# Attention and expert layers in one kernel: the third chunk's value products moved three steps earlier in 17 of 48 units, and two small copies moved to VectorE

## The chip, the cores and the metric

The kernel runs on one core of a Trainium2 chip. The metric is the device time of one launch in microseconds (us); a measurement is the median over several runs. Engines are called by their names or as the profile writes them: PE is TensorE's matmul side, PEld its weight loads, DVE is VectorE, ACT is ScalarE, POOL is GpSimd, SP is SyncE, which only issues transfers here.

## What is computed

Attention with normalised queries and keys over 8 batches, 12 heads, 448 positions and a head width of 64, then a gated expert layer of 8 experts, each token going to one of them.

```python
q_n, k_n = (rmsnorm(q, g_q), rmsnorm(k, g_k))
scores = scale * np.matmul(q_n, k_n.transpose(0, 1, 3, 2))
scores = scores - np.max(scores, axis=-1, keepdims=True)
attn = np.exp(scores)
attn = attn / (np.sum(attn, axis=-1, keepdims=True) + 1e-09)
attn_out = np.matmul(attn, v)
...
e_idx = np.argmax(x @ w_gate + modality_bias[modality_id], axis=1)
h = np.maximum(x[mask] @ w1[e], 0.0)
out[mask] = gate_w[mask, None] * (h @ w2[e])
```

The change touches the attention part alone.

## The kernel before, in words

**Units and steps.** The attention runs over 48 units (`NU`), a unit being two heads of one batch. The order of all work is written out by hand: a table `plan`, filled by `put(n, ...)`, says at which step `n` a piece is issued, and one loop walks the steps. A unit has seven steps, so `n = 7 * i + j` with the unit `i` and the step `j` from 0 to 6. The order in which a step's pieces are called is the order on each engine, and each engine runs its own in that order; the only freedom left at run time is how long an engine waits for a semaphore.

**What a step does.** The 2 x 448 positions of a unit's keys make seven chunks of 128 rows. In step `j`, `st(i, j)` (line 1012) multiplies chunk `j` of the keys with all queries into a bank of PSUM from the pool `ps_s`, which has two banks, and ACT turns the bank into exponentials (`A.activation(... Exp)`, line 1023). The third score product after a given one overwrites the bank of the first, so it has to wait for that exponential. Chunk 3 holds the last 64 rows of the first head and the first 64 of the second and takes four matmuls instead of two. In the same step `sa` (line 981) makes a chunk of a coming unit's scores, in the chunk order 3, 0, 1, 2, 4, 5, 6, only for their row maxima: DVE reduces each (`V.tensor_reduce`, line 994), again over two banks (`ps_a`). Step 3 and step 0 of the next unit also transpose queries and keys of a coming unit (`tr`, line 902): four PE transposes, a rounding copy by ACT, and a difference by DVE that waits for that copy; ACT then lays rounded rows into the operands, by four copies that come right after the exponential of step 4.

**The value products.** `av(u, c)` (line 1051) multiplies the exponentials of unit `u` with its values, during the steps of unit `i = u + 1`. Chunks `c` = 0, 1 and 2 are pairs of products, one for each head, on one half of the array's columns each; each product is recorded as two PE matmuls, so a pair is four of them. Chunk 3, shared by the heads, is one product over the full array, from a block-diagonal copy of the values.

```python
PLAN = {..., 'av': (1, 1, 4, 6), ...}
put(NJ * (u + 1) + (AVJ[c] if u < NU - 2 else min(AVJ[c], 6)), "av", u, c)
```

So chunks 0 and 1 are issued in step 1, chunk 2 in step 4 and chunk 3 in step 6. In step 4 there may follow `sums` (line 1078; after every odd `u`) or `gates` (line 1087; after every fourth `u`, here 8, 12, ... 40), eight matmuls of 32 columns each, four at a time side by side; and then `xt` (line 1122), four transposes. ACT empties the gates' bank before the exponential of step 5.

**The shared values.** `values(u)` (line 1064) fills the block-diagonal operand for chunk 3 by two copies of 64 x 64 within SBUF. It is called at the end of step 2 of unit `u + 1`, so on its engine it stands between step 2 and step 3.

**Other work around it.** POOL normalises queries and keys (two products of 1.05 us in a row at about step 2 or 3) and adds up exponentials; DVE also finishes `xt` (line 1131), and in every sixth unit the routing of a batch (`route_top`, line 1163, six small operations after step 4's reduction).

Of the kernel before, what the change touches and what calls it, by code (L numbers as in the profile page):

```python
# [21 lines left out]
NJ = 7  # L22
NP = H // 2
NU = B * NP
# [42 lines left out]
def kernel(  # L67
# [15 lines left out]
    V, A, G = (Deferred(e, n) for e, n in ((nc.vector, "op"), (nc.scalar, "act"), (nc.gpsimd, "dma")))  # L83
# [352 lines left out]
    def view(t, off, p, *dims):  # L436
        n = 1
        for d in dims:
            n *= d
        a = t[:p, off : off + n]  # L440
        if len(dims) > 1:
            ax = " ".join("abcd"[: len(dims)])
            a = a.rearrange(f"p ({ax}) -> p {ax}", **dict(zip("abcd"[1:], dims[1:])))
        return a
# [27 lines left out]
    vd_b = [view(at_l, 8 * DM - 128 * (i + 1), 128, 128) for i in range(2)]  # L472
# [336 lines left out]
    if True:  # L809
# [8 lines left out]
        HB = {}  # L818
# [244 lines left out]

        def values(u):
            for h, r in enumerate((LO, HI)):
                A.copy(vd_b[u % 2][r, 64 * h : 64 * h + 64], HB[u // 3]["v"][r, u % 3, 3])

        def avcopy(u):
            t = T[u]
# [305 lines left out]
        def put(n, *what):  # L1375
            plan.setdefault(n, []).append(what)

        P = PLAN
        AVJ, XTJ, XTE, SMJ, LAJ, RCJ = (P[x] for x in ("av", "xt", "xte", "sm", "la", "rc"))
# [7 lines left out]
        def xt_at(u):  # L1387
            if u < NU - 8:
                return NJ * (u + 6) + XTJ
            return NJ * (NU - 2 + (u - NU + 8) // 2) + XTE[u % 2]  # L1390

        def when(what, u):
            return P["first"].get((what, u), NJ * u - P[what])

        for u in range(NU):
            for j in range(NJ):
                jj = ((0, 1, 2, 4, 5, 6, 3) if u < P["early"] else (3, 0, 1, 2, 4, 5, 6))[j]
                put(when("sa", u) + j * (P["sastep"] if u == 0 else 1), "sa", u, jj)
            put(when("mt", u), "mt", u)
            if u < NU - 1:  # L1400
                for c in range(4):
                    put(NJ * (u + 1) + (AVJ[c] if u < NU - 2 else min(AVJ[c], 6)), "av", u, c)
            put(xt_at(u), "xt", u)
            if u % 2:
                put(NJ * (u + 1) + (SMJ if u < NP * (B - 2) else P["sml"]), "sums", u - 1)
            if u % 4 == 3:
                put(NJ * (u + 2) + (LAJ if u < NP * (B - 2) else min(LAJ, 4)), "gates", u // 4)
                put(NJ * (u + 2) + (RCJ if u < NP * (B - 2) else min(RCJ, 6)), "recips", u // 4)
            put(when("tk", u), "tr", u, 1)
            put(when("tq", u), "tr", u, 0)  # L1410
            put(when("nq", u), "norm", u, 0)
            put(when("nk", u), "norm", u, 1)
            put(when("sk", u), "sq", u, 1)
            put(when("sq", u), "sq", u, 0)
            if ("rs", u) in P["first"]:
                put(when("rs", u), "rs", u // 3, P["rs0"].get(u, 0), u % 3 + 1)
            elif u > 8 and u % 3 == 2:
                put(when("rs", u), "rs", u // 3, 0, 3)
            if 5 < u < 10:
                put(when("ld", u), "load", u)  # L1420
            elif u > 9 and u % 2 == 0:
                put(when("ld", u) - 1, "load", u, 2, (0,))
                put(when("ld", u) + 1, "load", u, 2, (1,))

        for n in range(P["start"], NJ * NU):
# [63 lines left out]
            if 0 <= i < NU and j in CSJ:  # L1489
                h = CSJ.index(j)  # L1490
# [20 lines left out]
            if i > 0 and j == 2:  # L1511
                values(i - 1)
            if i == NU - 1 and j == 4:
                values(i)
# [45 lines left out]
        u, g = NU - 1, NU // 4 - 1  # L1560
# [187 lines left out]
```

## Time and profile before

| what | value |
|---|---|
| median of 3 runs | 1034.41 us (1032.71 to 1034.77) |
| the profiled execution | 1034.98 us |
| its span in the trace | 1033.3 us |
| PE busy | 1013.8 us, 98% of the span |
| PE weight loads busy | 818.9 us, 79% |
| DVE, ACT, POOL busy | 743.5, 709.0, 715.9 us (72%, 69%, 69%) |
| granted TensorE clock | 0.998 of full speed |
| attention units | from about 26 to 540 us of the span |

The profiled execution is 1.7 us longer than the span of its instructions, and 0.6 us above the median of the runs. In the 40 slices of the page PE stands at 9 tenths nearly throughout, and ACT and DVE at 7 to 9 tenths up to the middle of the span, so busy shares alone don't tell what a shorter PE step would bring: a busy PE is one that has matmuls in flight. The trace's timeline, with the start of each matmul, tells more.

### The profile page before, as it was taken

The numbers are of one execution on the slowest core, as the hardware profiler recorded it, in microseconds if no ns is written. First come the engines' busy times: TensorE is split into PE (matmuls) and PEld (weight loads), VectorE is DVE, ScalarE is ACT, GpSimd is POOL, SyncE is SP. The second block draws the span as 40 slices with busy tenths as digits, with TensorE's granted clock in tenths as the row PEclk, the third lists the DMA queues.
The fourth block names the chain that finished last, engine by engine and source line by source line (L and its number), as shares of the span: only waits on it lengthen the run. The fifth ranks groups of instructions, "written<-read, shape, count | busy, mean of one in ns | idle before, by whom it ended". The sixth has DMA issues, their size and how long they took to land. (4 is left out here: it accounts for less than half of the span.)

```text
span 1033.3 us, 18863 instructions
## 1 busy us (share of the span) xinstructions
PE 1013.8 (98%) x6462; PEld 818.9 (79%) x6462; DVE 743.5 (72%) x1260; ACT 709.0 (69%) x1379; POOL 715.9 (69%) x747
## 2 busy tenths in 40 slices
PE   9899999999999999999989999999999999999997
PEld 7655666666666666656559999999999999999995
DVE  6777888887888788886667986755685567556740
ACT  7897999889999899888655555545554455545531
POOL 7788798989788887889856646865545554565361
PEclk9999999999999999999999999999999999999999
DMA  8776667868677786766748506144572342234162
GB/s 197 187 170 138 153 141 183 178 141 185 160 168 162 160 186 148 167 116 126 228 121 286 94 20 195 32 123 123 150 279 66 119 123 79 65 105 123 40 210 92
DMA packets 147900, 148.20 MB, mean 143 GB/s; under 512 B 72702, under 2 KB 137682, under 8 KB 147284
## 3 DMA queue, kind: packets, MB, share of 16 engines
q1 hardware_dynamic: 122398, 105.08, 43.0%
q0 software_dynamic: 25328, 41.82, 12.8%
q8 instruction: 53, 0.87, 0.4%
q14 instruction: 51, 0.42, 0.2%
q10 hardware_dynamic: 70, 0.02, 0.0%
HBM read 150.31 MB, written 33.39 MB: 178 GB/s over the span
## 5 line engine op out<-in xcount | busy, mean ns | idle before, releaser
L609 PE MATMUL ph<-xw,w1w 128*128 128x256 f32 x2016 | 246.1, 284 | 1.7 <-ACT at_w2lw L52 0.8
L609 PEld LDWEIGHTS ph<-xw,w1w 128*128 128x128 f32 x2016 | 243.9, 192 | 3.3 <-issue 1.1
L52 DVE TENSOR_REDUCE at_hlw<-sa 128x1 f32<-128x448 f32 x336 | 205.1, 619 | 26.3 <-PE sa L991 24.7
L1019 PE MATMUL st<-w1w 128*128 128x448 f32 (+1 forms) x480 | 183.5, 432 | 2.4 <-ACT at_w2lw L52 1.1
L52 POOL DMA_INDIRECT r<-in_moe_w_dram,tb_w x60 | 84.0, 1399 | 53.4 <-DVE w1w L52 38.1
L52 ACT ACTIVATE hhw<-ph 128x512 fp32r<-128x512 f32 x56 | 33.5, 597 | 121.2 <-PE ph L609 121.2
L639 PE MATMUL py<-w2lw,hhw 128*128 128x384 f32 x448 | 113.8, 335 | 0.0
L52 ACT ACTIVATE r2w<-st 128x448 f32<-128x448 f32 x168 | 91.0, 544 | 32.8 <-PE st L1019 26.6
L52 DVE TENSOR_TENSOR w1w<-r,w1w 128x768 fp32r<-128x768 f32 x112 | 103.9, 958 | 11.0 <-ACT w1w L52 9.9
L991 PE MATMUL sa<-w1w 128*128 128x448 f32 (+1 forms) x288 | 108.0, 375 | 3.6 <-DVE at_hlw L52 3.3
L52 POOL DMA_INDIRECT r2w<-in_moe_w_dram,tb_vi x48 | 50.0, 1041 | 84.7 <-DVE w2lw L52 75.7
L52 ACT CAST w1w<-xw 64x448 fp32r<-64x448 f32 x188 | 105.8, 563 | 3.7 <-issue 1.4
L52 DVE TENSOR_TENSOR w2lw<-r2w,w2ha 128x1536 fp32r<-128x1536 f32 x28 | 49.1, 1757 | 81.0 <-ACT w2ha L52 81.0
L1019 PEld LDWEIGHTS st<-w1w 128*128 128x128 f32 (+1 forms) x480 | 86.1, 190 | 25.5 <-issue 10.7
L1019 PE MATMUL st<-w1w,w2ha 65*128 65x448 f32 x288 | 100.5, 369 | 0.0
L52 POOL TENSOR_TENSOR r2w<-r2w 128x448 f32<-128x448 f32 (+1 forms) x72 | 82.9, 1152 | 24.0 <-DVE r2w L52 15.1
L52 ACT ACTIVATE at_w2lw<-st 128x448 f32<-128x448 f32 x168 | 90.6, 544 | 12.1 <-PE st L1019 6.9
L52 POOL TENSOR_TENSOR xrw<-r,at_hlw 112x512 f32<-112x512 f32 x95 | 97.6, 1047 | 0.5
L52 ACT CAST w1w<-r 128x768 fp32r<-128x768 f32 x112 | 95.3, 904 | 0.1
L52 ACT ACTIVATE yw<-py,ltn 128x384 f32<-128x384 f32 x55 | 29.3, 578 | 79.1 <-PE py L639 75.5
L639 PEld LDWEIGHTS py<-w2lw,hhw 128*128 128x128 f32 x448 | 80.9, 188 | 0.0
L52 POOL TENSOR_TENSOR r2w<-r2w,at_w2lw 64x448 f32<-64x448 f32 (+1 forms) x48 | 54.7, 1140 | 31.3 <-DVE r2w L52 15.7
(302 smaller groups left out, 2208.1 us busy)
## 6 DMA issues: line engine op xcount, KB each, us to landing
w1w<-xw SPq DMA_DIRECT2D x216, 112.0 KB
xg<-xrw SPq DMA_DIRECT2D x14, 768.0 KB
xrw<-xg SPq DMA_DIRECT2D x56, 192.0 KB
r<-in_q_dram SPq DMA_DIRECT2D x19, 448.0 KB
r<-in_k_dram SPq DMA_DIRECT2D x19, 448.0 KB
w2ha<-xw SPq DMA_DIRECT2D x72, 112.0 KB
w1w<-w1w SPq DMA_DIRECT2D x48, 112.0 KB
r2w<-in_v_dram SPq DMA_DIRECT2D x24, 224.0 KB
```

What stands on the lines that cost most here:

```text
L52: return fn(*a, **kw)
L609: PE.matmul(ps[:, i], lhsT=lt_, rhs=rt_[:, c], start=n == 0, stop=n == 17)
L639: PE.matmul(ps[n][:, :384], lhsT=lt_[:, j, 128 * t : 128 * t + 128], rhs=rt_[:, 384 * n : 384 * n + 384], start=j == 0 and m == 0, stop=j ...
L991: PE.matmul(ps[:, :S], lhsT=t["qq"][r, h, a : a + 128], rhs=t["kk"][h][r], start=True, stop=True)
L1019: PE.matmul(ps[:, :S], lhsT=l, rhs=t["qq"][:, h] if first else t["ql"][0:65, h], start=first and (j != 3 or h == 0), stop=not first and (j ...
```

## The change

```diff
         def values(u):
             for h, r in enumerate((LO, HI)):
-                A.copy(vd_b[u % 2][r, 64 * h : 64 * h + 64], HB[u // 3]["v"][r, u % 3, 3])
+                copy = V.tensor_copy if 8 <= u < 42 else A.copy
+                copy(vd_b[u % 2][r, 64 * h : 64 * h + 64], HB[u // 3]["v"][r, u % 3, 3])
...
                 for c in range(4):
-                    put(NJ * (u + 1) + (AVJ[c] if u < NU - 2 else min(AVJ[c], 6)), "av", u, c)
+                    aj = AVJ[1] if c == 2 and u % 2 == 0 and 8 <= u < 41 else AVJ[c]
+                    put(NJ * (u + 1) + (aj if u < NU - 2 else min(aj, 6)), "av", u, c)
```

In the 17 units 8, 10, ... 40 chunk 2's four PE matmuls move from step 4 to step 1, behind those of chunks 0 and 1. For the 34 units 8 to 41 the two copies of the shared values move from ACT to DVE, at the same place between steps 2 and 3. Nothing else moves.

Three places show it. All rows are of the products of unit 26 in the steps of unit 27, the number behind a name being the scheduler's own (`av` the value products, `st` the scores, `sa` those for the maxima, `tr` and `xt` transposes). On PE, before:

```order
L1061 MATMUL av_3860<-r2w 64x448 x4
L1002 MATMUL mt_3865<-idn,at_hlw 7x128
L1019 MATMUL st_2_3875<-w1w 128x448 x2
L991 MATMUL sa_1_3878<-w1w 128x448
L1019 MATMUL st_3_3891<-w1w 128x448 x4
L991 MATMUL sa_2_3896<-w1w 128x448
L910 MATMUL tr_0_3898<-idn,xrw 128x112 x4
L1019 MATMUL st_4_3906<-w1w 128x448 x2
L991 MATMUL sa_4_3909<-w1w 128x448
L1061 MATMUL av_3860<-r2w 64x448 x2
L1127 MATMUL xt_3913<-idn,at_hhw 112x128 x4
```

and with the change:

```order
L1061 MATMUL av_3860<-r2w 64x448 x6
L1002 MATMUL mt_3867<-idn,at_hlw 7x128
L1019 MATMUL st_2_3877<-w1w 128x448 x2
L991 MATMUL sa_1_3880<-w1w 128x448
L1019 MATMUL st_3_3893<-w1w 128x448 x4
L991 MATMUL sa_2_3898<-w1w 128x448
L910 MATMUL tr_0_3900<-idn,xrw 128x112 x4
L1019 MATMUL st_4_3908<-w1w 128x448 x2
L991 MATMUL sa_4_3911<-w1w 128x448
L1128 MATMUL xt_3913<-idn,at_hhw 112x128 x4
```

The two products of chunk 2 have left the place between `sa_4` and `xt` and lengthen the group in front of `mt`; the rows between are the same.

On ACT, from the exponential of step 2 (`st_2`) to that of step 5, with the change (before, one row more stood behind the first: `COPY at_w2lw<-r2w 64x64 x2`):

```order
L52 ACTIVATE at_w2lw<-st_2_3877 128x448
L52 ACTIVATE at_w2lw<-st_3_3893 128x448
L52 CAST xw<-tr_0_3900 128x448
L52 ACTIVATE at_w2lw<-st_4_3908 128x448
L52 CAST w1w<-xw 64x448
L52 CAST xw<-xw 64x64
L52 CAST w1w<-xw 64x448
L52 CAST xw<-xw 64x64
L52 ACTIVATE at_w2lw<-st_5_3937 128x448
```

The four casts still stand between the exponentials of step 4 and of step 5.

On DVE, the same steps with the change (before, the row with COPY was not there):

```order
L52 TENSOR_REDUCE at_hlw<-sa_1_3880 128x1
L52 COPY at_w2lw<-r2w 64x64 x2
L52 TENSOR_REDUCE at_hlw<-sa_2_3898 128x1
L52 TENSOR_TENSOR w1w<-tr_0_3900,xw 128x448
L52 TENSOR_REDUCE at_hlw<-sa_4_3911 128x1
L52 TENSOR_REDUCE ra_3925<-lo_3808 112x4
```

The two copies now stand between the maxima of chunks 1 and 2, and what follows them is as before.

## Rows read from the trace of the kernel before

**Rows 1.** Busy time by stretch: us, then PE, PEld, DVE, ACT, POOL, PEclk, DMA.

```profile
240.00:320.00 80.00, 80.00 (x443) 50.02 (x443) 67.07 (x129) 72.34 (x169) 67.98 (x74) 1.00 0.75 170
```

**Rows 2.** Timeline of PE in unit 27: start, length, operation, count.

```profile
314.25 1.72 PE L1061 MATMUL av<-r2w 128*64 128x448 f32 x8
315.91 0.28 PE L1002 MATMUL mt<-idn,at_hlw 128*7 128x128 f32 x1
...
318.49 0.37 PE L991 MATMUL sa<-w1w 128*128 128x448 f32 x1
318.79 0.97 PE L1061 MATMUL av<-r2w 128*64 128x448 f32 x4
319.69 0.65 PE L1127 MATMUL xt<-idn,at_hhw 128*112 128x128 f32 x4
...
321.21 0.37 PE L991 MATMUL sa<-w1w 128*128 128x448 f32 x1
321.41 0.91 PE L1057 MATMUL av<-r2w,at_w2lw 128*128 128x448 f32 x2
321.81 0.71 PE L1019 MATMUL st<-w1w 128*128 128x448 f32 x1
...
322.56 0.37 PE L986 MATMUL sa<-xw 128*128 128x448 f32 x1
```

**Rows 3.** Timeline of PE at the attention's end, chunks 0 to 2 together.

```profile
536.77 2.48 PE L1061 MATMUL av<-at_w2lw 128*64 128x448 f32 x12
539.18 1.02 PE L1057 MATMUL av<-at_w2lw 128*128 128x448 f32 x2
```

**Rows 4.** Timeline of PE in unit 25, where gates follow.

```profile
297.04 0.37 PE L991 MATMUL sa<-w1w 128*128 128x448 f32 x1
...
298.24 0.57 PE L1090 MATMUL sm<-at_hhw,wg 128*32 128x448 f32 x2
...
299.13 0.65 PE L1127 MATMUL xt<-idn,at_w2hb 128*112 128x128 f32 x4
```

**Rows 5.** Timeline of ACT in unit 27, from step 4's exponential to step 5's.

```profile
318.69 0.55 ACT L52 ACTIVATE at_w2lw<-st 128x448 f32<-128x448 f32 x1
...
320.45 0.24 ACT L52 CAST xw<-xw 64x64 fp32r<-64x64 f32 x1
320.84 1.16 ACT L52 ACTIVATE at_w2lw<-st 128x448 f32<-128x448 f32 x2 [0.15 <-PE st L1019]
```

**Rows 6.** Timeline of PE in unit 37, step 4's score product.

```profile
422.47 0.47 PE L1019 MATMUL st<-w1w 128*128 128x448 f32 x1
```

**Rows 7.** Timeline of ACT in unit 37, step 2's exponential.

```profile
421.90 0.52 ACT L52 ACTIVATE at_w2lw<-st 128x448 f32<-128x448 f32 x1
```

**Rows 8.** Timeline of DVE in unit 27.

```profile
316.85 0.63 DVE L52 TENSOR_REDUCE at_hlw<-sa 128x1 f32<-128x448 f32 x1
317.87 0.62 DVE L52 TENSOR_REDUCE at_hlw<-sa 128x1 f32<-128x448 f32 x1 [0.40 <-PE sa L991]
318.82 0.62 DVE L52 TENSOR_TENSOR w1w<-tr,xw 128x448 fp32r<-128x448 f32 x1 [0.33 <-ACT xw L52]
...
321.60 1.15 DVE L52 TENSOR_REDUCE at_hlw<-sa 128x1 f32<-128x448 f32 x2
322.67 0.67 DVE L52 SCALAR_TENSOR_TENSOR r2w<-at_w2lw,half 128x448 f32<-128x448 f32 x1
```

**Rows 9.** The routing's first small operation on DVE, 80 to 430 us: count, ns, times.

```profile
L52 DVE TENSOR_REDUCE ra<-lo x5: 182/184/186, 152.4 to 403.5; 112x4 f32<-112x32 f32 x5
```

**Rows 10.** Groups of DVE copies after 1000 us: count, busy us, mean ns.

```profile
L52 DVE COPY xrw<-idn 32x32 f32<-32x32 f32 x4 | 0.4, 283 | 0.0
```

**Rows 11.** Timeline of DVE in unit 19: the operation with two SBUF inputs.

```profile
238.60 1.60 DVE L52 SCALAR_TENSOR_TENSOR r2w<-at_w2lw,half 128x448 f32<-128x448 f32 x1
```

**Rows 12.** Timeline of POOL at that time, and in unit 27.

```profile
238.58 1.14 POOL L52 TENSOR_TENSOR r2w<-r2w,at_w2lw 64x448 f32<-64x448 f32 x1
...
316.51 2.05 POOL L52 TENSOR_TENSOR xrw<-r,at_hlw 112x512 f32<-112x512 f32 x2
318.52 1.14 POOL L52 TENSOR_TENSOR r2w<-at_w2lw 128x448 f32<-128x448 f32 x1
```

## Prediction

> **What bounds the kernel now.** I first read the busy time by stretch: in the middle of the attention PE is busy for the whole of 80 us, while ACT stands at 72 and DVE at 67 [rows 1]. So PE is the bound there, and a shorter PE sequence would shorten the kernel one for one, as long as the others keep up. A busy PE only has matmuls in flight, though, so I went on to the timeline and read start against start. The change touches 17 units, in each at two places: the group of value products in step 1 and the one in step 4. The third view is the timeline of ACT and DVE beside it, for what follows PE there: 72 of 80 us is little room for an engine that has to answer PE within two score banks.
>
> **What the moved products save on PE.** Unit 27 stands for the plain units, in which no gates follow.
> - Step 4 before: from the maxima product to the transposes behind the value products 318.49 to 319.69, 1.20 us [rows 2]. A maxima product followed by a product over the full array takes 321.21 to 321.41, 0.20 [rows 2]. Taking the group out frees 1.00 us.
> - Step 1: eight matmuls take 314.25 to 315.91, 1.66 [rows 2]. Twelve of the same kind, at the end of the attention, take 536.77 to 539.18, 2.41 [rows 3]. So the third pair costs 0.75 there.
> - Net 0.25 us less: what is saved is one way into the half-array form and out of it again.
>
> Where gates follow (9 of the 17: 8, 12, ... 40) the way from the maxima product to the gates' first matmul is the same 1.20, 297.04 to 298.24 [rows 4]. But the gates split the array too, into quarters. Their own way in, straight from a full-array product, the trace of these steps doesn't show; the value group's is 318.49 to 318.79, 0.30 instead of 0.20 [rows 2]. The bounds are 0.20 and 0.30, the saving 0.25 or 0.15. I take 0.15, since both are the same switch from whole to split. If PE were all, the sum would be 8 x 0.25 + 9 x 0.15 = 3.35 us less, at most 17 x 0.25 = 4.25.
>
> **What the later steps 2 to 4 cost.** All between the two places now starts 0.75 later, while what follows step 4 is to start 0.25 earlier. ACT and DVE lose 1.00 us between them in every such unit. In unit 27 they follow PE closely: DVE waited 0.40 for PE, then 0.33 for ACT's copy of the transposes [rows 8]. So they shift by the whole 0.75 (bounds 0 and 0.75; 0 only with a backlog that would hide the shift, and these waits exclude one).
> - ACT: step 4's exponential goes from 318.69 to 319.44. The four casts end at 320.45 + 0.24 = 320.69 and left 0.15 us of idle time before step 5's exponential [rows 5]; now they end at 321.44. Step 5's exponential, 0.55 long like step 4's [rows 5], runs until about 322.01.
> - The next unit's first score product overwrites that bank. A product waiting for such an exponential starts 0.05 behind it: 421.90 + 0.52 = 422.42, and 422.47 [rows 6, 7]. So it starts at 322.06, where PE would be ready at 321.81 - 0.25 = 321.56 [rows 2]. **PE stalls 0.50 and the unit ends up 0.25 longer than before, not 0.25 shorter.**
> - DVE: its difference of the transposes goes from 318.82 to 319.57. Behind it no idle time is printed up to the two reductions at 321.60 [rows 8], since this is a unit with the six small routing operations. The first ends at 322.22, now 322.97. The maxima product at 322.56 [rows 2] needs that bank and could start at 323.02: 0.46 later than before, not 0.25. The routing falls into 5 of the 8 plain units, the first at 152.4 and the last at 403.5 [rows 9]. In the other three DVE has that much less to do, and the 0.25 stands.
> - Where gates follow, they take 298.24 to 299.13, 0.89 us of PE [rows 4], ahead of step 5. That covers nearly all of the 1.00, so the saving of 0.15 stays.
>
> **The two copies.** ACT loses two short copies between the exponentials of steps 2 and 3. In the moved units ACT waits there for PE, which is later now, so this can't shorten the chain above; in the others nothing on PE waits for ACT. I cost it at nothing; its cover is PE's own full row, and if ACT were the bound in those units, it would be a gain. DVE gains two copies of 64 x 64. The trace has no such copy; the nearest is one of 32 x 32, four of which keep DVE busy for 0.4 us, mean 283 ns [rows 10]. So two cost 0.2 to 0.6 us; I take 0.3. They stand in the 0.40 us in which DVE waited for PE [rows 8], which hides them, and the later PE adds 0.36 behind them in the moved units. That is zero as long as they don't have to wait.
>
> **Sum.** 5 x 0.45 + 3 x 0.25 - 9 x 0.15 = 2.25 + 0.75 - 1.35 = **1.65 us more**. On the profiled execution (1034.98) that is 1036.63; that one lies 0.57 above the median of the runs, so the median becomes 1034.41 + 1.65, about **1036.0 us**. A step that moves 17 groups then moves the kernel by less than 0.2% (2.07 us), about what a measurement of this kernel can tell from no change.
>
> **Rivals.**
> - *Faster: ACT keeps up.* If step 5's exponential in the plain units ends by 321.51, PE finds its bank free at 321.56 and all savings stay: 3.35 us less, 1031.1 us. It decides at a lateness of ACT of 0.25 instead of 0.75. For it speaks that ACT loses 0.5 us of copies and had 0.15 idle [rows 5]. Against it: the copies stand ahead of the place where ACT waits for PE, and the four casts can't pass each other.
> - *Slower: DVE's copies wait for POOL.* An operation of DVE with two inputs in SBUF took 1.60 us beside a POOL operation of 1.14 that had begun just before [rows 11, 12], and 0.67 where POOL left it alone [rows 8]. If a copy within SBUF is held up likewise, then in the plain units with routing: DVE is free for the copies at 316.85 + 0.63 + 0.75 = 318.23, POOL's second product runs until 318.56, and the addition behind it begins at once, 1.14 long [rows 12]. If the first copy goes in between and the second waits for the addition, DVE reaches chunk 2's reduction at about 320.06 and the difference at 320.68 instead of 319.57. The 1.1 us go through to the maxima product of the next unit: 5 x 1.1 more, 1034.41 + 1.65 + 5.5 = 1041.5 us. It decides at a delay of the copies of about 0.7 us; a single wait of 0.33 stays hidden. The page "SBUF — State Buffer" of the Trainium skill (section "Who interferes with whom") has the rule for it: a copy can use both of DVE's ports, and then it and a GpSimd instruction exclude each other, whoever comes second waiting for the whole of the other. By that rule the first copy waits 0.33 at this place; whether the second lets POOL's addition go first it doesn't say.
> - *No effect at all.* If the end of the attention is set by something other than PE, both gains and losses upstream vanish there: 1034.4 us. Rows 1 speak against it for the stretch of the change; what comes after 500 us I have not followed step by step.
>
> **How the numbers follow.** The forecast has 0.52. Its own range is 1034.8 to 1037.4 (the 0.15 of the gates between 0.15 and 0.25, the DVE term between 0.25 and 0.55), and since 1036.5 is 0.2% above the median, about a third of it counts as slower. ACT keeping up has 0.15, the waiting copies 0.25, no effect 0.08. Faster by over 0.2%: 0.12, most of the first rival. Slower by over 0.2%: a third of the forecast (0.17) and nearly all of the copies' (0.23), 0.40. The rest, 0.48, is within 0.2%. The range goes from 1032.2, two thirds of the way to ACT keeping up, to 1042.0, behind the waiting copies.
>
> **What would show it.** Right: twelve value matmuls of 2.41 us in step 1 of 17 units, and none in step 4 there; in the eight plain ones PE idle by about 0.5 us ahead of the next unit's first score product, with ACT's exponential of step 5 ending 0.05 before it; no such stall where gates follow; DVE's copies of 0.2 us or so each in the gap ahead of chunk 2's reduction. Wrong: no stall at those first score products (then it is faster), or copies of over 0.7 us and stalls at the maxima products, in units that the change of order doesn't touch too (then it is slower).

## The result and the profile after

| kernel | median | runs | ratio to the kernel before |
|---|---|---|---|
| before, in the same series | 1033.99 us | 4 | |
| changed | 1048.02 us (1047.31 to 1048.88) | 4 | 1.0136, interval 1.0123 to 1.0149 |

The change costs 14 us, beyond the end of the predicted range (1042.0). The profiled execution took 1047.36 us, its span is 1045.5 us.

The stretch of [rows 1] shows the kind of loss: PE is no longer busy throughout, DVE has gone from 67.07 to 75.42 of 80 us, and ACT and POOL have become less busy. So DVE is late, and not because ACT or POOL work more.

```profile
240.00:320.00 80.00, 76.58 (x412) 47.68 (x413) 75.42 (x135) 64.44 (x143) 64.86 (x72) 0.98 0.69 158
```

The groups of DVE between 100 and 500 us, kept apart by shape, name what is new: 68 copies of 64 x 64 with 55.3 us between them. The prediction had 0.3 us for a pair, 10.2 us for 34. (After the count: busy us and mean ns; in the second fence, least, median and greatest ns, and the first and last start.)

```profile
L52 DVE COPY at_w2lw<-at_w2lw 64x64 f32<-64x64 f32 x36 | 32.6, 905 | 0.3
L52 DVE COPY at_w2lw<-r2w 64x64 f32<-64x64 f32 x32 | 22.7, 709 | 0.2
```

```profile
L52 DVE COPY at_w2lw<-at_w2lw x36: 174/691/3503, 137.3 to 490.2; 64x64 f32<-64x64 f32 x36
L52 DVE COPY at_w2lw<-r2w x32: 176/408/3535, 127.7 to 455.9; 64x64 f32<-64x64 f32 x32
```

A copy that isn't held up takes 0.17 to 0.19 us; the two longest took 3.50 and 3.54. The longest stands in the steps of unit 26, in which the change moves no value products. DVE there:

```profile
310.27 1.14 DVE L52 TENSOR_REDUCE at_hlw<-sa 128x1 f32<-128x448 f32 x2
311.33 3.74 DVE L52 COPY at_w2lw<-r2w 64x64 f32<-64x64 f32 x2
315.10 0.19 DVE L52 TENSOR_SCALAR rs<-sp 112x32 f32<-112x32 f32 x1
...
315.71 0.62 DVE L52 TENSOR_TENSOR lg<-sp,rs 112x64 f32<-112x64 f32 x4
```

POOL at that time:

```profile
310.69 0.96 POOL L1235 DMA_INDIRECT l_d<-ltk,posi  x1 [0.16 <-issue]
311.67 2.05 POOL L52 TENSOR_TENSOR xrw<-r,at_hlw 112x512 f32<-112x512 f32 x2
313.67 1.13 POOL L52 TENSOR_TENSOR r2w<-r2w 128x448 f32<-128x448 f32 x1
314.97 0.96 POOL L1235 DMA_INDIRECT l_d<-ltk,posi  x1 [0.17 <-issue]
```

and PE:

```profile
313.75 0.55 PE L1084 MATMUL sm<-at_w2lw,sel 128*32 128x448 f32 x2
316.48 0.62 PE L1128 MATMUL xt<-idn,at_hhw 128*112 128x128 f32 x4 [2.18 <-DVE lg L52]
```

The first copy starts at 311.33 and ends at 314.86, 0.05 after the last of three POOL products (313.67 + 1.13); the second copy then takes 0.19. PE's transposes overwrite a bank that the routing's products (`lg`) on DVE still have to read, and wait 2.18 us. Comparing the ends in the two timelines, every one of the 42 copies that took over 0.3 us ends 0.044 to 0.059 us behind the end of a POOL instruction; the 26 others took at most 0.25. In 31 of the 34 units at least one of the two waited.

That pause has a second price. In stretches of 2 us (the clock is the third number from the end) it runs from 314 to 316, and then the granted clock falls to the lower of its two levels and comes back after 320. Unit 26 is 3.90 us longer than before (14.83 against 10.93, from score product to score product), 1.7 more than the pause:

```profile
314.00:316.00 2.00, 0.30 (x4) 0.00 (x0) 1.89 (x7) 0.34 (x2) 1.81 (x3) 1.00 0.32 74
316.00:318.00 2.00, 1.52 (x8) 1.42 (x9) 2.00 (x6) 0.12 (x1) 1.92 (x2) 0.76 0.01 0
318.00:320.00 2.00, 2.00 (x5) 1.12 (x4) 2.00 (x5) 1.40 (x3) 0.31 (x1) 0.50 0.25 57
```

Who PE waited for from 80 to 560 us (us in all, times, longest), before:

```profile
PE sa L991 <- DVE at_hlw L52: 0.8, 1, 0.8
...
PE sa L986 <- DVE at_hlw L52: 0.4, 1, 0.4
```

and after:

```profile
PE sa L991 <- DVE at_hlw L52: 5.5, 13, 1.1
PE sa L986 <- DVE at_hlw L52: 2.9, 6, 0.6
PE xt L1128 <- DVE lg L52: 2.2, 1, 2.2
...
PE xt L1128 <- DVE at_hlw L52: 0.8, 2, 0.4
```

In these rows, behind DVE, that is 11.4 us in place of 1.2. The 10.2 us more are most of the 14, and the lower clock comes on top. Neither trace has a wait of PE for a transfer in this stretch.

Unit 27, the plain unit of [rows 2, 5, 8], has its twelve value products in one group now:

```profile
322.38 2.48 PE L1061 MATMUL av<-r2w 128*64 128x448 f32 x12
324.79 0.28 PE L1002 MATMUL mt<-idn,at_hlw 128*7 128x128 f32 x1
```

That is 2.41 from start to start, as in [rows 3].

### The profile page after: what moved, and what is told of

Its sections match the earlier page's. It is cut to its first block, busy times and chain, and to the rows that moved or that the text cites. A ratio compares the mean times of both kernels' runs of the same rounds, so it can differ in the third digit from the quotient of the medians.

```text
span 1045.5 us, 18864 instructions
## 1 busy us (share of the span) xinstructions
PE 1017.8 (97%) x6462; PEld 819.5 (78%) x6462; DVE 790.1 (76%) x1328; ACT 693.1 (66%) x1311; POOL 709.7 (68%) x747
## 5 line engine op out<-in xcount | busy, mean ns | idle before, releaser
L991 PE MATMUL sa<-w1w 128*128 128x448 f32 (+1 forms) x288 | 110.3, 383 | 6.4 <-DVE at_hlw L52 5.9
```

Source lines behind the costliest of these rows:

```text
L991: PE.matmul(ps[:, :S], lhsT=t["qq"][r, h, a : a + 128], rhs=t["kk"][h][r], start=True, stop=True)
```

## The experiments

Kernels of one block of the table ran on the same chip and share the runs of the kernel before.

| run | what it is | median, us | runs | ratio, 95% interval |
|---|---|---|---|---|
| before | | 1035.02 | 23 | |
| e1_move_only | 17 moves, copies on ACT | 1038.76 | 12 | 1.0033, 1.0021 to 1.0045 |
| e2_copies_only | no move, copies on DVE | 1052.87 | 5 | 1.0172, 1.0157 to 1.0188 |
| e3_reduce_form | the change, copies as reductions | 1038.07 | 6 | 1.0032, 1.0020 to 1.0045 |
| e4_move_gates | 9 moves, copies on ACT | 1033.93 | 12 | 0.9985, 0.9977 to 0.9994 |
| before | | 1034.75 | 35 | |
| e5_sums_too | 25 moves, copies on ACT | 1036.03 | 12 | 1.0010, 0.9992 to 1.0027 |
| e6_gates_reduce | 9 moves, copies as reductions | 1035.94 | 12 | 1.0003, 0.9990 to 1.0016 |
| e7_reduce_only | no move, copies as reductions | 1036.24 | 12 | 1.0007, 0.9994 to 1.0019 |
| e8_not18 | 16 moves, copies on ACT | 1035.99 | 12 | 1.0009, 0.9994 to 1.0024 |
| before | | 1035.36 | 9 | |
| e9_copies_ahead | no move, copies on DVE elsewhere | 1043.04 | 5 | 1.0072, 1.0058 to 1.0086 |
| e10_sums_look | e5 again | 1036.85 | 1 | |
| before | | 1033.36 | 21 | |
| e11_sums_gap | 19 moves, copies on ACT | 1031.69 | 11 | 0.9984, 0.9975 to 0.9993 |
| e12_sums_gap37 | 16 moves, copies on ACT | 1031.52 | 11 | 0.9979, 0.9970 to 0.9988 |

For the middle of the attention, lengths of single units tell more than a total. A unit's length here is the time in PE's timeline from its first score product (line 1019) to that of the next unit, in us of the profiled executions. Units 19 and 27 are plain, 21 and 29 have gates; nothing is moved in 12, 20, 26 and 28.

| unit | before | e1 | e2 | e3 | e4 | changed |
|---|---|---|---|---|---|---|
| 12 | 11.16 | 11.47 | 12.57 | 11.47 | 11.16 | 12.57 |
| 19 | 9.63 | 9.97 | 10.03 | 9.72 | 9.63 | 10.02 |
| 20 | 10.49 | 10.25 | 10.50 | 10.32 | 10.49 | 10.53 |
| 21 | 10.54 | 14.19 | 10.49 | 11.95 | 10.33 | 10.35 |
| 26 | 10.93 | 10.88 | 14.59 | 10.93 | 10.88 | 14.83 |
| 27 | 9.63 | 9.87 | 9.65 | 9.87 | 9.63 | 10.01 |
| 28 | 10.49 | 10.80 | 10.85 | 10.79 | 10.49 | 10.80 |
| 29 | 11.21 | 11.01 | 11.21 | 11.01 | 11.01 | 11.01 |

**The move alone.** The change with its first part undone:

```diff
-                copy = V.tensor_copy if 8 <= u < 42 else A.copy
+                copy = A.copy
```

> Only the value products move, in the 17 units; ACT keeps the copies of the shared values. Theory A (the copies on DVE wait for POOL and make DVE late for PE): the 13.6 us of the change are nearly gone, the time lies between 3.35 us under the kernel before (the PE saving alone) and 1.65 us over it (the sum forecast), with no DVE copies and no more PE idle time behind DVE than before. Theory B (it is the move: ACT's step 5 exponential comes late in the moved units): about as slow as the change, 10 us or more over the kernel before, PE idle time before the first score products. Theory C (DVE has no room for 0.4 us more work in a unit, whether it waits or not): as theory A here.

Measured: 3.4 us over the kernel before, 2.2 to 4.7 by the interval. Most of the change's loss is gone with the copies, so theory B falls; but the move costs about twice the forecast's 1.65. The times lie in two groups, five of the twelve from 1035.95 to 1036.76 (0.9 to 1.7 over, near the forecast) and seven from 1038.62 to 1041.42; the profiled execution, 1041.28, is of the slower ones. In its profile the units behave as forecast. PE in units 27 and 28:

```profile
325.38 0.91 PE L1057 MATMUL av<-r2w,at_w2lw 128*128 128x448 f32 x2
326.34 0.47 PE L1019 MATMUL st<-w1w 128*128 128x448 f32 x1
326.65 0.36 PE L1019 MATMUL st<-w1w,w2ha 65*128 65x448 f32 x1
327.30 0.47 PE L986 MATMUL sa<-xw 128*128 128x448 f32 x1 [0.28 <-DVE at_hlw L52]
```

and ACT's exponentials of steps 5 and 6:

```profile
325.75 0.98 ACT L52 ACTIVATE at_w2lw<-st 128x448 f32<-128x448 f32 x2
```

The next unit's first score product comes 0.96 behind the last value products, where [rows 2] has 0.40: a stall of 0.56 that ends just behind the first of the two exponentials. The maxima product then waits 0.28 for DVE. What the sum didn't have stands above all in unit 21, which is 3.65 us longer (unit 42 is 1.04 longer too, and units 37 to 39 together 0.96 shorter):

```profile
249.00 0.71 PE L1019 MATMUL st<-w1w 128*128 128x448 f32 x1
250.60 0.47 PE L1019 MATMUL st<-w1w,w2ha 65*128 65x448 f32 x1 [0.89 <-DMA w1w<-xw]
...
252.89 0.55 PE L991 MATMUL sa<-w1w 128*128 128x448 f32 x1 [0.81 <-DMA w1w<-xw]
253.37 4.01 PE L1061 MATMUL av<-r2w 128*64 128x448 f32 x12
```

PE waits twice for transfers within SBUF that SP issues: for the row of maxima (line 1007), and for a half of an operand that goes to the other half of the partitions (line 923). Behind that the twelve value products take 4.01 us, at a granted clock of 0.50 from 254 to 256:

```profile
252.00:254.00 2.00, 1.20 (x4) 0.48 (x5) 1.21 (x3) 1.99 (x5) 2.00 (x3) 0.77 0.98 255
254.00:256.00 2.00, 2.00 (x8) 0.71 (x6) 0.59 (x2) 0.20 (x1) 1.77 (x2) 0.50 1.13 284
```

**The copies alone.** The other half, `aj = AVJ[c]` for all units:

> Only the copies move from ACT to DVE, in 34 units; the value products stay in step 4. Theory A (copies wait for POOL): 10 to 17 us over the kernel before (the change's 13.6 without what the move brought, which lay between 3.35 saved and 1.65 lost), with single copies of up to 3.5 us as in the change. Theory B (the move): within 1 us of the kernel before, or a little faster, since ACT loses 16 us of busy time. Theory C (DVE load): 10 to 17 us over, but also with copies that do not wait.

Measured: 17.8 us over, 16.2 to 19.5; the copies by themselves lose more than the whole change. The profile has single copies of up to 3.5 us here too, and units 26 and 12 lose as in the change. The move takes some 4 us off again. In the traces that isn't a cover in each moved unit: nearly all of it lies in units 14 and 15, 14.91 and 11.78 us long here against 10.93 and 10.20 with the change. PE waits 2.20 us for `lg` in unit 14 here, as 2.02 in unit 26, and the lower clock follows there too. So it hangs on where single copies meet POOL.

```profile
L52 DVE COPY at_w2lw<-at_w2lw x36: 177/872/2418, 137.4 to 493.4; 64x64 f32<-64x64 f32 x36
L52 DVE COPY at_w2lw<-r2w x32: 177/356/3540, 126.9 to 461.3; 64x64 f32<-64x64 f32 x32
```

**Another instruction at the same place.** The change, but with another instruction for the copies (outside units 8 to 41 ACT keeps them):

```diff
-                copy(vd_b[u % 2][r, 64 * h : 64 * h + 64], HB[u // 3]["v"][r, u % 3, 3])
+                dst, src = vd_b[u % 2][r, 64 * h : 64 * h + 64], HB[u // 3]["v"][r, u % 3, 3]
+                if 8 <= u < 42:
+                    V.tensor_reduce(out=dst, in_=src.rearrange("p (a b) -> p a b", b=1), op=ALU.max, axis=AX.X)
...
```

> The change as it is, but each of DVE's copies is written as a maximum over an axis of length 1: same data, same place in the order, same engine, another instruction. Theory A (a copy within SBUF is held up by POOL's products, a reduction is not: chunk reductions beside POOL took their usual 0.62 us): each takes about 0.2 us and does not wait, the time is within 1.5 us of the run that moves only the products. Theory C (DVE has no room for the work, 34 x 2 x 0.2 = 13.6 us of it): still 8 us or more over that run. Theory B (the move): as slow as the change.

Measured: as fast as the run that moves only the products (1.0032 and 1.0033). Same engine, same data, same place; yet none of the 68 takes more than 0.22 us, though 41 of them ran wholly within one of POOL's two-input operations (TENSOR_TENSOR):

```profile
L52 DVE TENSOR_REDUCE at_w2lw<-at_w2lw x36: 198/209/218, 136.8 to 477.2; 64x64 f32<-64x64 f32 x36
L52 DVE TENSOR_REDUCE at_w2lw<-r2w x32: 198/210/218, 127.2 to 445.2; 64x64 f32<-64x64 f32 x32
```

So DVE has room for the work here, and theory C falls. What costs is that a copy is held up by POOL and a reduction isn't. The page "SBUF — State Buffer" of the Trainium skill, section "Who interferes with whom", states both: a copy may use a pair of ports that DVE shares with GpSimd, a reduction on this chip never does. These rows agree.

The same form without any move:

> No value product moves; only the copies go to DVE, written as reductions over an axis of length 1. Beside the run with plain copies on DVE (17.8 us over the kernel before) only the form of 68 instructions differs. Theory A (the port that POOL holds): within 1 us of the kernel before. Theory C (load): 5 us or more over it.

Measured: 1.0007, with 1 inside the interval. Against the 1.0172 of the copies, the form of 68 instructions is worth about 17 us.

**The same copies at another place.** No move; DVE makes the copies in `csum`, ahead of its weighted sum, and no longer behind step 2:

```diff
             if h in CSV:
+                if 8 <= u < 42:
+                    values(u)
                 V.scalar_tensor_tensor(out=c2, ...)
...
-            if i > 0 and j == 2:
+            if i > 0 and j == 2 and not 9 <= i < 43:
                 values(i - 1)
```

> As the run with the copies alone on DVE (plain copies, no product moved), but DVE makes them just ahead of its weighted sum for the column sums (line 1034's scalar_tensor_tensor) instead of behind step 2. In the kernel before POOL had run out of work at 18 of these 36 places, since its next addition waits for that sum. Theory A (a copy waits only while POOL runs): at about half of the places the copies take 0.2 us each, and the loss over the kernel before falls from 17.8 us to between 4 and 10. Theory C (DVE's load, wherever it stands): still 15 us or more.

Measured: 7.5 us over, 6.0 to 8.9, inside theory A's span. The copies' busy time falls to 22.7 us, and 56 of the 68 are short, under 0.3 us (28 in e2). So the same copies are held up less often at this place, and cost less.

```profile
L52 DVE COPY at_w2lw<-r2w 64x64 f32<-64x64 f32 x32 | 13.0, 405 | 0.2
L52 DVE COPY at_w2lw<-at_w2lw 64x64 f32<-64x64 f32 x36 | 9.7, 270 | 0.2
```

How much of the 7.5 us is theirs isn't shown: PE's longest wait in this trace, 2.39 us in unit 39, is one for a transfer (us in all, times, longest):

```profile
PE st L1019 <- DMA w1w<-xw: 2.6, 2, 2.4
```

**The move where gates follow.** Copies on ACT, `u % 4 == 0` in place of `u % 2 == 0`:

> The move only in the nine units in which gates follow in step 4 (8, 12, ... 40); ACT keeps all the copies. By the step of the prediction: 9 x 0.15 = 1.35 us under the kernel before (bounds 0.15 to 0.25 each: 1.35 to 2.25), no new PE stall at the first score products. If the saving lies in the gates units and the loss in the plain ones, this is faster than the run with all 17 moved; if ACT keeps up everywhere, it is slower than that run by 8 x 0.25 = 2 us. Rival (the later steps 2 to 4 make a DVE reduction late here too): no gain or a loss.

Measured: 1.5 us under the kernel before (0.9985; 0.6 to 2.4 by the interval), where 1.35 was forecast. The unknown price, the gates' own way in, is now in the trace, 0.30 from start to start (295.85 to 296.15), the bound that the prediction took:

```profile
295.85 0.37 PE L991 MATMUL sa<-w1w 128*128 128x448 f32 x1
296.15 0.57 PE L1091 MATMUL sm<-at_hhw,wg 128*32 128x448 f32 x2
```

With the copies as reductions on top:

> The move in the nine gates units, and DVE's copies written as reductions over an axis of length 1 in all 34 units. In the run with all 17 moved this form was as fast as with ACT's copies (ratios 1.0032 and 1.0033). Theory A: no waits on POOL, so the same time as the gates alone with ACT's copies, within 0.5 us; a little less if ACT's 16 us of busy time that go had been late for PE anywhere. Theory C (DVE has no room): over the gates alone by 2 us or more.

Measured: 1.0003, so the gain is gone, against the expectation; the 1.9 us over the run of the gates alone are close to the 2 that theory C named. The profile has one place for it: PE waits for POOL once, in unit 42, and the clock is at 0.50 from 480 to 482 behind it; the unit is 14.74 us long, 10.68 with ACT's copies. The run e3 has such a wait there too, of 1.3 us. Why POOL is late there with reductions on DVE wasn't tried.

```profile
PE sm L1087 <- POOL at_w2hb L52: 2.0, 1, 2.0
```

**The wait for a transfer.** All moves but that of unit 18's values (`and u != 18`):

> All moved units but one (the values of unit 18, in step 1 of unit 19, stay in step 4); ACT keeps the copies. The run that moved all 17 was 3.5 us over the kernel before where the sum of the prediction gave 1.65, and its profile has one wait for a DMA in unit 21, 3.65 us long with the lower clock behind it, that the kernel before does not have. Theory F (unit 19 being 0.3 later pushes the transfer of unit 21's operands into busy DMA queues): without that move the wait is gone, and the time is 1.4 to 3.6 us under that run, at 0 to 2 us over the kernel before. Rival G (the shift of all units before it, or chance, does it): the wait is there as well, and the time is within 0.7 us of that run.

Measured: 0.9 us over the kernel before, and 2.5 us under the run with all 17 (1.0009 against 1.0033), as theory F has it. Eleven of the twelve times lie below 1037.5, five of e1's. In the profile unit 21 is as short as in the run of the gates alone (10.33), and the forecast's sum without this unit (1.65 less 0.25) lies inside the interval. So most of what e1 had over the forecast goes with one move of 17 and the wait for a transfer behind it. The move alone doesn't settle it: of the runs with all 17, e3 has such waits in unit 21 too (0.71 and 0.42 us), but in the changed kernel's trace the unit takes 10.35 and waits for no transfer.

**More moves.** Column sums of 32 columns follow in the even units, as gates do elsewhere (`u % 4 != 2`, copies on ACT):

> The move in the nine units in which gates follow in step 4 and also in the sixteen in which the column sums follow there (values of odd units, 9 to 39): 25 units in all, none of the plain ones; ACT keeps the copies. Theory D (a quarter-array group behind the value products covers the later steps, as the gates did: the run of the gates alone gave 0.20 us in each): 25 x 0.20 = 5 us under the kernel before, about 3.5 under the run of the gates alone. Rival E (DVE is fuller in the units with sums, since the routing's logits run there: its reductions come 0.75 later and the maxima products wait): no gain over the gates alone, or a loss of up to 16 x 0.3 = 5 us.

> The kernel with 25 moved units once more, for its trace: its times lay between 1030.38 and 1040.89 us, and the profiled one was the lowest. Theory H (with PE ahead of its old pace a score product now and then finds its operand's transfer not landed, and the lower clock behind the pause doubles the price): an execution of 1034 us or more shows one or two waits of PE for a DMA, each over 0.7 us, with a stretch at 0.5 to 0.9 of the clock behind it, and units without them as short as before. Rival J (many small waits for DVE): the units with sums are each some tenths longer.

Measured: no gain in the median (1.0010), but times from 1030.38 to 1040.89, more spread than with any other kernel. Traces of two executions, the lowest and one of 1036.85, tell why. In the lowest, units with sums are mostly 0.14 to 0.20 us shorter (unit 12: 11.02, unit 28: 10.35), as theory D has it. They are just as short in that of 1036.85, against rival J; there unit 19 is 5.22 us longer, behind one wait for a transfer:

```profile
226.91 0.66 PE L1019 MATMUL st<-w1w 128*128 128x448 f32 x2
230.98 0.44 PE L991 MATMUL sa<-w1w 128*128 128x448 f32 x1 [3.41 <-DMA w1w<-xw]
```

The clock is 1.00 from 225 to 230 and 0.68 from 230 to 235, the DMA share 0.93 and 0.62. SP had issued the last of the transfers of this kind by 225.61, and behind them a write of 672 KB at 226.30 and a load of 224 KB at 226.97; what holds the transfer up until 230.84 isn't settled.

**A version that beats both.** So the last two keep the old order around that place (values of units 13 to 20), and the second also at the end (37 to 40):

```diff
-... c == 2 and u % 2 == 0 and 8 <= u < 41 ...
+... c == 2 and u % 4 != 2 and 8 <= u < 37 and not 13 <= u < 21 ...
```

> The gates and sums units as in the run with 25 moves, but not the values of units 13 to 20 (so steps as before in units 14 to 21, ahead of and where the wait for a transfer stood): 19 moves, none of them in a plain unit; ACT keeps the copies. Theory H (the long wait for a transfer around units 19 to 21 is what made that kernel's median 1036.03 with a lowest of 1030.38): it becomes rare, the times lie close together, and 19 moves at 0.16 to 0.20 us give 3 to 3.8 us under the kernel before. Rival K (any gain upstream brings PE onto those transfers): times as wide as before, and no gain in the median.

> As the kernel above, and without the moves of the values of units 37 to 40 (units 38 to 41), where in the run with 25 moves one unit got 0.7 us longer and three got 0.1 to 0.4 shorter: 16 moves. Theory H and those units: the same as the kernel above within 0.5 us. Rival: what is lost in unit 42 after the gates-only move (0.44) goes too, and it is 0.5 us or more faster.

Measured: 0.9984 and 0.9979, both faster, with times that lie close together (1030.86 to 1033.75 and 1030.40 to 1033.37). Theory H holds for the spread. The size falls short: 1.7 us instead of 3 or more in the first. In its profile units 39 and 42 are 0.69 and 0.74 us longer than before and take back 1.4 us of what the moved units save. Whether leaving out the last four moves helps isn't decided: the second is ahead by 0.2 us in the medians, and its unit 42 is no shorter (11.17 against 10.98). The second is 2.2 us under the kernel before and 1.5% under the changed one.

## Why the prediction was wrong

- **The two copies: the step that failed.** "That is zero as long as they don't have to wait" was put in for all 34 units, and they had to wait in 31. No row shows the 0.36 us of further cover that it counted on in the moved units. A copy that isn't held up takes 0.17 to 0.19 us, inside the 0.1 to 0.3 that the prediction's bound gives for one. What was missing is 42 us of waiting on DVE (55.3 less 68 x 0.19), of which 10.2 us reached PE as waits behind DVE. By the runs it is nearly 11 us against e1 (1.0136 and 1.0033), and 13 against e8 (1.0009), whose profile, like the changed kernel's, has no long wait for a transfer.
- **The rival had the mechanism but was priced in 5 of the 34 units.** It counted only the plain units with routing, because those have no idle time on DVE behind the copies. But copies met POOL's products in 31 of the 34 units, moved or not, and in 24 of them the two waited over 0.8 us together, twice the 0.40 us that were to hide them. The row that it rested on, a sum of 1.60 us in place of 0.67 [rows 8, 11], was a warning for every place at which POOL runs back to back [rows 12], not for one unit.
- **The price of a wait was bounded too low.** 1.1 us stood for one POOL operation; in 19 of the 42 waits of the changed kernel more than one POOL instruction ended before the copy did, and they went up to 3.5 us. The pause of 2.18 us that one of them brought PE was followed by the lower clock.
- **The sign that the prediction named for being slower is what the trace shows**: copies of over 0.7 us and stalls at the maxima products (`sa`), also in units like 12 and 24, in which nothing is moved.
- **The move's terms were about right in the units.** Gates: 0.15 forecast, 0.20 in unit 29, 0.10 and 0.05 over a pair of units like 25 and 26. ACT's lateness: a stall of 0.50 forecast, 0.56 measured, 0.25 more per plain unit forecast, 0.24 measured. With routing, 0.45 more forecast, 0.55 measured over units 27 and 28. Without routing, 0.25 forecast; units 19 and 20 together show 0.34 less 0.24, 0.10: the lateness is caught up in the next unit.
- **What the sum of the move lacked** is the transfers. It moved steps against engines alone, and didn't ask when the operands that SP sends within SBUF land. In the profile of e1 that made one unit 3.65 us longer, and by the medians of e1 and e8 it costs 2 to 3 us. It is no part of the changed kernel's 14 us as far as its profile shows, since PE waits for no transfer there.
- **The first rival** (ACT keeps up) is excluded by the stall of 0.56. That nothing happens at all is excluded by the intervals.

## What to carry to other kernels

Before work is moved to a less busy engine, look at which of its instructions POOL can hold up: here a copy within SBUF cost 0.19 us or up to 3.5, and the same copy written as a reduction over an axis of length 1 cost 0.20 to 0.22 always. A wait that the trace shows at one place is to be priced at every place where the same two engines meet, not where it was found. On a kernel whose TensorE is fully busy a pause can cost more than itself (here 3.90 us for one of 2.18), and a step that shortens PE is worth only as much as the transfers ahead of it have slack: ask for both before adding up savings.

## What was not expected of the hardware

- A waiting copy isn't let in at every boundary between two POOL instructions. The one at 311.33 came while POOL issued a transfer and sat through the three products behind it, the first of which started 0.34 us after the copy; others got in at the next boundary. The copies at 181.11 and 181.30 ran within such an issue of a transfer and took 0.18 and 0.19 us. The rule of "SBUF — State Buffer" in the Trainium skill (section "Who interferes with whom"), that whoever issues first has the pair for its whole instruction, fits with the ends of all 42 waits; that the copy which started first came last at 311.33, it doesn't tell, and no run here explains it.
- Two pauses of PE, of 0.89 us up to 250.60 and 0.81 us up to 252.89, in unit 21 of the run with the moves alone, were followed by a clock of 0.50 over 2 us, as a single one of 2.18 was.
